# Attention and two MoE layers on one core: a new order of the attention's tasks, in which TensorE keeps its kind of tile

## The chip, the cores and the metric

The kernel runs on one core of one Trainium2 chip. The metric is device time in microseconds (us), from the start to the end of one execution. Five engines work side by side, each with an instruction queue of its own that it executes in order: TensorE (PE, with its weight loads PEld), VectorE (DVE), ScalarE (ACT), GpSimd (POOL) and SyncE (SP), which in this kernel issues nearly all the transfers. They wait for each other through semaphores.

## The reference

Attention over 4 batches, 8 heads, 576 positions and 64 columns a head, mixed with a memory read through phi, and then two MoE layers on the 2304 tokens. All of it is float32.

```python
scores = np.where(causal, -1e9, scale * q @ k.T)          # causal: strictly above the diagonal
a = np.exp(scores - scores.max(-1)); a /= a.sum(-1) + 1e-09
local = a @ v
q_p = phi(q)                                              # x + 1 where x > 0, else exp(x)
mem_out = (q_p @ M_prev) / (q_p @ z_prev + 1e-06)
g = 1 / (1 + np.exp(-beta))
attn = g * mem_out + (1 - g) * local
x = attn.transpose(0, 2, 1, 3).reshape(2304, 512)
g1 = x @ w_gate; x = (g1 * sigmoid(g1) * (x @ w_val)) @ w_out
h = x @ w_in; out = piecewise(h) @ moe2_w_out              # (h + 1)**2 / 4 between -1 and 1
```

## The kernel before

The program has two parts with a planner each. The first part is the attention, beside the decoding of the first twelve weight units and the early gate and value products of the first three groups of 512 tokens. The second part has the rest of the first MoE layer and the whole second one. A `Plan` collects tasks (engine, duration, priority, what they depend on, which buffers they take), plays them through with an estimated duration for each, and emits the instructions in the order in which its play started them. So every engine's order is fixed when the program is built, and on the chip an engine waits at its next instruction however much later work is ready.

The attention works on 16 pairs of heads (4 batches x 4 pairs, `pair`, L380). For a pair, SyncE loads K with the last 64 positions of Q (`kn`, four DMAs), Q (`qn`, three) and V (`vn`, three), and once a batch z (three) and M (two). TensorE transposes K and Q (`tk`, `tm`, `tq`, L496 to L512), and makes the scores: for the four blocks of 128 rows the scores of both heads side by side, each head on 64 rows of the array (L610, 128, 256, 384 and 512 columns), and the last 64 positions of both heads on the whole array (`qk4`, L640). VectorE masks them and takes the row minimum (L620, L647), ScalarE takes the exponential with its row sum (L627, L658), VectorE adds up and inverts the sums (`r`, L682 and L686), GpSimd multiplies each block by them (L695), and TensorE transposes the scaled blocks on the whole array (`t4`, `t03` to `t01`, `t13` to `t11`, L706 to L746). ScalarE or VectorE copies each transposed bank from PSUM (`copies`, L410 and L417; the table `COPY` says which of them). Beside this, phi of Q is made by ScalarE and VectorE (L529 to L536), its product with z and the sum by GpSimd (L541 to L562), and TensorE transposes it (`tp`, `tp4`, L568). At the end `av0` (L774 and L781, 320 columns a product) and `av1` (256) multiply both heads' M and V, each head on 64 columns of the array, and `x` is written as two float32r parts (L785, L788) and stored.

When a group of 512 tokens has all its pairs stored, its `xh` is loaded again, and the early products `mm<-xh` (L1030, 144 instructions a group) run on the whole array, between the attention's own.

What sets the order are the numbers of `ORDER` and `FIRST_ORDER`, one for each kind of task and added to 100 times the pair's number; `EARLY` for the weight units; `GROUP_AT` and `X_AT` for the early products; and the planner's costs. Of the tasks that are ready and have their buffers, an engine takes the one with the lowest number (`Plan.order`, L154). VectorE's operations that share a port with GpSimd (`port=True`) are played as waiting for it, and all of GpSimd's as waiting for them:

```python
if eng == "DVE" and found["port"]:
    dur += max(0, ends["POOL"] - now)
    ends["DVE"] = now + dur
elif eng == "POOL":
    dur += max(0, ends["DVE"] - now)
    ends["POOL"] = now + dur
```

Of the kernel before, what the change touches and what calls it, by code (L numbers as in the profile page):

```python
# [30 lines left out]
FIRST_PAIRS = 3  # L31
AB, RB1, RB0 = 3, 2, 2
# [4 lines left out]
EARLY = (58464.4906, 31703.8921, 46024.3389, 15376.5891, -67113.9713, 33679.2323, 24516.8779, 64604.3348, 926.9641, 15791.9914, 50392.9186, 34533.2938)  # L37
# [8 lines left out]
GROUP_AT, X_AT = (58101.0278, -5262.7152, 78550.5678), (81713.5868, 13183.1344, -54614.9227)  # L46
# [20 lines left out]
    "load": -13097.6716, "load_v": 55113.6308, "load_z": -18855.7456, "load_M": 38998.1826, "tk": 51026.1438,  # L67
    "tm": -96571.9864, "tq": -19483.9254, "tk.cp": -45495.7399, "tm.cp": -7125.2447, "tq.cp": -15756.7918,
    "min": -42893.5849, "exp": -31473.534, "phi": 250.0948, "w": -55573.7784, "fold": -2977.3896, "nrm":
# [9 lines left out]
}  # L79
FIRST_ORDER = {  # L80
    "load": -35369.7195, "load_v": 11324.0126, "load_z": -39943.6113, "load_M": -1948.6302, "tk": 57244.7662,
    "tm": -20365.3582, "tq": 43517.0557, "tk.cp": -28665.4259, "tm.cp": -32651.252, "tq.cp": -2666.435, "min":
    -17582.8303, "exp": -34662.1945, "phi": 32542.1117, "w": -33941.3334, "fold": -21505.6005, "nrm":
# [9 lines left out]
}  # L93
# [179 lines left out]
def c_pool(n):  # L273
    return 0.835 * n + 250
# [1350 lines left out]
```

## Time and profile before

| | us |
|---|---|
| median of 3 runs (1055.95 to 1058.71) | 1056.94 |
| the profiled execution | 1055.26 |
| its span, first to last instruction | 1053.5 |
| TensorE busy in the span | 1037.8 (99%) |
| VectorE busy | 672.7 (64%) |
| ScalarE busy | 569.5 (54%) |
| GpSimd busy, all of it in the attention | 216.0 (21%) |

The rows further below come from this execution. An engine is busy while it has an instruction in execution; matmuls are pipelined and the ends of theirs are modelled, so that the start of one group to the start of the next tells more of TensorE than the busy time does. "PEclk" is the granted clock of TensorE as a share of full speed. "[1.22 <-DMA qn]" behind a row is how long the engine was idle before it, in us, and what ended that. A score or `av` product appears as two records in the trace, a transposition as one.

### The profile page before, as it was taken

What the parts mean: (1) busy time and instruction counts of PE and PEld (TensorE: products, weight loads), DVE (VectorE), ACT (ScalarE), POOL (GpSimd) and SP (SyncE); (2) the same over time, 40 slices, a digit from 0 to 9 for tenths busy, and PEclk for the clock granted to TensorE, in tenths of its full rate; (3) what the DMA queues carried; (4) which work ended last, traced back from release to release, by engine and by line L of the source; (5) the groups of instructions that cost most, each with busy time, mean ns of one, the idle gap of its engine ahead of it and who ended that gap; (6) DMA issues with size and microseconds to landing.
All of it is one profiled execution on the core that took longest, in us unless ns stands there. A gap on an engine that the chain in (4) does not pass through costs nothing.

```text
span 1053.5 us, 17539 instructions
## 1 busy us (share of the span) xinstructions
PE 1037.8 (99%) x6096; PEld 862.9 (82%) x6096; DVE 672.7 (64%) x1547; ACT 569.5 (54%) x1282; POOL 216.0 (21%) x301
## 2 busy tenths in 40 slices
PE   6899999999999999999999999999999999999998
PEld 4666766767788898888888889999999999899997
DVE  5899787761124677968777776843585767643443
ACT  6898887883222445525353444655564555544443
POOL 7898998992000000000000000000000000000000
PEclk8999999999999999999999999999999999999999
DMA  7794564224596699765869696999679878855422
GB/s 167 181 241 121 169 172 137 91 89 156 199 301 202 214 343 401 227 234 203 315 236 333 208 341 228 362 409 414 245 267 336 310 266 292 285 208 189 166 81 80
DMA packets 172072, 248.10 MB, mean 236 GB/s; under 512 B 72913, under 2 KB 99537, under 8 KB 171985
## 3 DMA queue, kind: packets, MB, share of 16 engines
q1 hardware_dynamic: 170078, 245.64, 68.5%
q10 hardware_dynamic: 1906, 1.35, 0.4%
q8 instruction: 48, 0.79, 0.3%
q14 instruction: 40, 0.32, 0.1%
HBM read 165.15 MB, written 81.79 MB: 234 GB/s over the span
## 4 chain that ended last, share of the span: by engine, by line
PE 95%; ACT 1%; DMA 1%; SPq 1%; POOL 1%; issue 0%; DVE 0%; ACTq 0%; POOLq 0%
PE mm L1030 28%; PE acc L1558 19%; PE mm L1279 17%; PE acc L1374 14%; PE av L781 4%; PE s L610 3%; PE t L729 2%; PE av L774 2%; PE s L640 1%; PE t L746 1%; PE t L706 1%; PE tp L568 1%; DMA qn<-in_q_dram 1%; PE tk L499 1%; ACT a L627 0%; SPq L431 0%
## 5 line engine op out<-in xcount | busy, mean ns | idle before, releaser
L1558 PE MATMUL acc<-wu,h 128*128 128x512 f32 x864 | 210.3, 391 | 0.0
L1030 PE MATMUL mm<-xb,wu 128*128 128x512 f32 (+1 forms) x1008 | 201.1, 359 | 0.0
L1030 PEld LDWEIGHTS mm<-xb,wu 128*128 128x128 f32 x1008 | 170.1, 189 | 28.3
L1558 PEld LDWEIGHTS acc<-wu,h 128*128 128x128 f32 x864 | 157.4, 189 | 29.3
L1279 PE MATMUL mm<-xb,wu 128*128 128x256 f32 x1188 | 153.9, 283 | 0.0
L1279 PEld LDWEIGHTS mm<-xb,wu 128*128 128x128 f32 x1188 | 150.0, 192 | 3.6 <-ACT mm L1350 0.3
L1374 PE MATMUL acc<-h,wu 128*128 128x512 f32 (+1 forms) x720 | 151.8, 368 | 0.0
L1374 PEld LDWEIGHTS acc<-h,wu 128*128 128x128 f32 x720 | 125.8, 189 | 22.4
L1191 ACT CAST h<-t 128x512 fp32r<-128x512 f32 (+1 forms) x140 | 80.6, 579 | 91.3 <-PE acc L1374 37.3
L1194 DVE TENSOR_TENSOR h<-t,h 128x512 fp32r<-128x512 f32 (+1 forms) x140 | 88.3, 635 | 50.3 <-ACT h L1191 49.6
L1263 ACT ACTIVATE t<-mm,half 128x512 f32<-128x512 f32 (+1 forms) x80 | 51.7, 646 | 117.7 <-PE mm L1279 73.4
L1030 PE MATMUL mm<-xh,wu 128*128 128x512 f32 x432 | 107.5, 401 | 0.0
L695 POOL TENSOR_SCALAR a<-a,r,OGP 128x512 f32<-128x512 f32 (+3 forms) x144 | 98.8, 698 | 15.0 <-DVE r L686 10.6
L1269 DVE SCALAR_TENSOR_TENSOR t<-mm,t 128x512 f32<-128x512 f32 (+1 forms) x80 | 50.9, 637 | 75.5 <-ACT t L1266 75.2
L1030 PEld LDWEIGHTS mm<-xh,wu 128*128 128x128 f32 x432 | 79.4, 188 | 18.0 <-issue 0.5
L1078 ACT COPY gvo<-mm 128x512 f32<-128x512 f32 (+1 forms) x80 | 43.0, 543 | 92.6 <-PE mm L1030 81.9
L627 ACT ACTIVATE a<-a,mn 128x256 f32<-128x256 f32 (+3 forms) x128 | 70.9, 556 | 4.8 <-DVE mn L620 4.5
L847 ACT ACTIVATE wA<-raw 128x512 f32<-128x512 f32 x64 | 43.0, 672 | 41.1 <-DMA raw<-in_moe_w_out_dram 18.7
L417 DVE COPY R<-t 128x256 f32<-128x256 f32 (+3 forms) x96 | 35.8, 416 | 41.7 <-PE t L746 35.7
L620 DVE CUSTOM_DVE_ANT_0 a<-s,mask 128x256 f32<-128x256 f32 (+3 forms) x128 | 56.8, 481 | 8.5 <-PE s L610 8.1
L908 ACT CAST wu<-wA 128x512 fp32r<-128x512 f32 x56 | 34.6, 617 | 30.8 <-DVE wA L877 22.4
L852 DVE TENSOR_SCALAR wA<-wA 128x512 f32<-128x512 f32 x68 | 31.0, 456 | 31.0 <-ACT wA L847 30.9
(132 smaller groups left out, 1407.9 us busy)
## 6 DMA issues: line engine op xcount, KB each, us to landing
xb<-ys SPq DMA_DIRECT2D x69, 512.0 KB, 7.7
park<-wu SPq DMA_DIRECT2D x40, 512.0 KB, 7.1
wu<-park SPq DMA_DIRECT2D x40, 512.0 KB, 6.8
xb<-xs SPq DMA_DIRECT2D x32, 512.0 KB, 7.4
gv<-gv SPq DMA_DIRECT2D x32, 512.0 KB, 7.1
ys<-yo SPq DMA_DIRECT2D x31, 512.0 KB, 5.7
gv<-gvo SPq DMA_DIRECT2D x60, 256.0 KB, 3.4
raw<-in_moe_w_out_dram SPq DMA_DIRECT2D x28, 512.0 KB, 6.4
```

What stands on the lines that cost most here:

```text
L620: nc.vector.tensor_tensor_reduce(a, st[f"s{h}{c}"][:, 0:kl], self.mask0[:, 512 - kl:512], -0.125, 3.0e38, ALU.add, ALU.min, mn[:, o:o + 1])
L627: nc.scalar.activation(a, a, AF.Exp, bias=mn[:, o:o + 1], scale=-1.0, accum_out=sm[:, o, 0:1])
L695: nc.gpsimd.tensor_scalar(a, a, st["mn"]["r"][:, o:o + 1], self.OGP[:, n, o:o + 1], op0=ALU.mult, op1=ALU.mult)
L847: nc.scalar.activation(f32(s["F"]), f32(words(s["raw"])[:, :, 1]), AF.Abs)
L1030: nc.tensor.matmul(out, kt_of(unit, pw, kt), x[kt][:, px, cols], start=(kt == 0 and i == 0), stop=(kt == KT - 1 and i == 2))
L1191: nc.scalar.copy(s["h"][:, 0], s["t"])
L1194: nc.vector.tensor_sub(s["h"][:, 1], s["t"], f32(s["h"][:, 0]))
L1263: nc.scalar.activation(mk_t(o), src(), AF.Relu, bias=half, scale=0.5)
L1269: nc.vector.scalar_tensor_tensor(o["t"], src(), 1.0, o["t"], op0=ALU.max, op1=ALU.min)
L1279: nc.tensor.matmul(out, pair["k"](k, pw, j), y["x"][piece][:, px, j], start=first and not (i or j), stop=last and j == 1 and i == 2, skip_ ...
L1374: nc.tensor.matmul(state[m][:, 0:n], l, r, start=(begin and i == 0), stop=(end and i == 2), skip_group_check=True)
L1558: nc.tensor.matmul(state[m], s["h"][:, px, m * P:(m + 1) * P], unit["w"][:, pw], start=(begin and i == 0), stop=(end and i == 2), skip_gro ...
```

## The change

The tables that set the attention's order have new numbers, and so have the copies' engines. The planner knows a kind of tile for each of TensorE's tasks (`form`: 1 for scores, 2 for `av`, 0 for the rest). With `stay` it takes, of the tasks that are ready, the first of the kind it is at, if its number is not more than `stay` above that of the first ready one of another kind; `stay` is 1e9. A change of kind costs 165 ns in the plan (`turn`), and the 150 ns that each score and `av` product cost beside its columns are gone. VectorE's operations on the shared port are now played in two ways: behind GpSimd's operations on two tensors (`port=True` there) they wait until one comes that has a single tensor, or none; behind the others as before. GpSimd's scalings cost 285 instead of 250 ns beside their columns, and a DMA's issue 640 instead of 600.

```diff
+STAY, TURN = 1.0e9, 165
-EARLY = (58464.4906, 31703.8921, 46024.3389, ...
+EARLY = (7014.831, 9462.3219, -44116.6461, ...
-GROUP_AT, X_AT = (58101.0278, -5262.7152, 78550.5678), (81713.5868, 13183.1344, -54614.9227)
+GROUP_AT, X_AT = (-13804.7284, -11763.634, 2577.9887), (-9395.3711, -14855.2931, -18112.8928)
 ORDER = {
-    "load": -13097.6716, "load_v": 55113.6308, "load_z": -18855.7456, "load_M": 38998.1826, "tk": 51026.1438,
+    "load": -6563.114, "load_v": -2708.1865, "load_z": -42493.462, "load_M": -15954.7577, "tk": -16212.2191,
...
-COPY = {"tk": "DVE", "tm": "ACT", "tq": "ACT", "tp": "ACT", "tp4": "ACT", "t4": "DVE", "t03": "ACT", "t02": "ACT",
-        "t01": "DVE", "t13": "DVE", "t12": "ACT", "t11": "ACT"}
+COPY = {"tk": "DVE", "tm": "ACT", "tq": "ACT", "tp": "DVE", "tp4": "ACT", "t4": "ACT", "t03": "DVE", "t02": "DVE",
+        "t01": "ACT", "t13": "ACT", "t12": "ACT", "t11": "ACT"}
...
-        t = self.add("SP", (600 if self.over else 530) * len(times), prio, fn, deps, uses, 0, behind)
+        t = self.add("SP", (640 if self.over else 530) * len(times), prio, fn, deps, uses, 0, behind)
...
-                skipped, found = [], None
+                skipped, found, best = [], None, None
                 while heap:
                     e = heapq.heappop(heap)
                     t = self.tasks[e[1]]
+                    if best is not None and t["prio"][0] > best["prio"][0] + self.stay:
+                        skipped.append(e)
+                        break
...
                     if all(len(free[k]) >= v for k, v in need.items()):
-                        found = t
-                        break
+                        if eng != "PE" or not self.stay or t["form"] == form:
+                            found = t
+                            break
+                        best = best or t
                     skipped.append(e)
+                if found is None and best is not None:
+                    found = best
+                    skipped.remove((best["prio"], best["n"]))
...
+                if eng == "PE":
+                    dur += self.turn * (found["form"] != form)
+                    form = found["form"]
...
+                if eng == "DVE" and found["port"]:
+                    if ends["row"] > now:
+                        shut = found
+                        continue
+                    dur += max(0, ends["POOL"] - now)
+                    ends["DVE"] = now + dur
+                elif eng == "POOL":
+                    if shut is not None and not found["port"]:
+                        ends["DVE"] = now + shut["dur"]
+                        begin(shut, now + shut["dur"])
+                        shut = None
+                    dur += max(0, ends["DVE"] - now)
+                    ends["POOL"] = now + dur
+                    if found["port"]:
+                        ends["row"] = now + dur
...
 def c_two(*cols):
-    return sum(4 * n / 2.4 + 5 for n in cols) + 150
+    return sum(4 * n / 2.4 + 6 for n in cols)
...
 def c_pool(n):
-    return 0.835 * n + 250
+    return 0.835 * n + 285
...
-            t_q = add("PE", c_two(kl), "qk", qk, [t_k, t_S], [*places, i_K, i_S, i_a[0, c], i_a[1, c]])
+            t_q = add("PE", c_two(kl), "qk", qk, [t_k, t_S], [*places, i_K, i_S, i_a[0, c], i_a[1, c]], form=1)
...
-                    [i_o, i_P, i_v, i_M, *(i_R1, i_R0)[rg]])
+                    [i_o, i_P, i_v, i_M, *(i_R1, i_R0)[rg]], form=2)
...
-                    slow={"PE": (15500, 1.7)})
+                    slow={"PE": (15500, 1.7)}, stay=STAY, turn=TURN)
```

TensorE, in the middle of the attention, before: the last transposition of one pair's scaled blocks (`t_2453`), then another pair's scores `s_...<-K,S` (both heads of 512, 384, 256 and 128 columns), with transpositions of scaled blocks (`<-ident,a`) and an early product `mm<-xh` among them.

```order
L729 MATMUL t_2453<-ident,a_2311 128x128 x3
L610 MATMUL s_2460<-K,S 128x512
L610 MATMUL s_2461<-K,S 128x512
L610 MATMUL s_2468<-K,S 128x384
L610 MATMUL s_2469<-K,S 128x384
L746 MATMUL t_2476<-ident,a_2322 128x128
L746 MATMUL t_2476<-ident,a_2317 128x128 x2
L1030 MATMUL mm<-xh,wu 128x512 x6
L610 MATMUL s_2500<-K,S 128x256
L610 MATMUL s_2501<-K,S 128x256
L610 MATMUL s_2508<-K,S 128x128
L610 MATMUL s_2509<-K,S 128x128
L746 MATMUL t_2515<-ident,a_2381 128x128
```

The scores of this pair stand in two runs, with whole-array work between. The same stretch of the pairs now, from a transposition on:

```order
L759 MATMUL t_2505<-ident,a_2349 128x128 x4
L640 MATMUL s_2514<-K,S 128x384
L640 MATMUL s_2515<-K,S 128x384
L640 MATMUL s_2522<-K,S 128x512
L640 MATMUL s_2523<-K,S 128x512
L640 MATMUL s_2533<-K,S 128x256
L640 MATMUL s_2534<-K,S 128x256
L640 MATMUL s_2543<-K,S 128x128
L640 MATMUL s_2544<-K,S 128x128
L1061 MATMUL mm<-xh,wu 128x512 x6
L540 MATMUL tq<-ident,qn 128x128 x4
```

All eight score products of a pair stand in one run, and the whole-array work before and behind them in one run each.

SyncE, behind the first pair's K, before: a weight unit (`raw`), z of the first batch (`zb`, `zh`), K of the second pair (`kn_1`) and its Q (`qn_289`).

```order
L842 DMA raw_267<-in_moe_w_gate_dram 128x4x256
L457 DMA zb_269<-in_z_prev_dram 128x512
L461 DMA zh_271<-in_z_prev_dram 64x4x64 x2
L431 DMA kn_1_195<-in_k_dram 128x4x64 x2
L439 DMA kn_1_195<-in_k_dram 64x2x64
L443 DMA kn_1_195<-in_q_dram 64x2x64
L431 DMA qn_289<-in_q_dram 128x4x64 x2
L446 DMA qn_289<-in_q_dram 128x1x64
```

Now the same queue has z of the first batch and the weight unit first, then z of the second batch (its last piece is the first row here), then V of three pairs (`vn`), and only then the second pair's K and Q (`qn_366`).

```order
L491 DMA zh_276<-in_z_prev_dram 64x4x64 x2
L461 DMA vn_0_197<-in_v_dram 128x4x64 x2
L469 DMA vn_0_197<-in_v_dram 64x2x64
L461 DMA vn_1_198<-in_v_dram 128x4x64 x2
L469 DMA vn_1_198<-in_v_dram 64x2x64
L461 DMA vn_2_199<-in_v_dram 128x4x64 x2
L469 DMA vn_2_199<-in_v_dram 64x2x64
L461 DMA kn_1_195<-in_k_dram 128x4x64 x2
L469 DMA kn_1_195<-in_k_dram 64x2x64
L473 DMA kn_1_195<-in_q_dram 64x2x64
L461 DMA qn_366<-in_q_dram 128x4x64 x2
L476 DMA qn_366<-in_q_dram 128x1x64
```

The second pair's Q moves from the 15th to the 27th DMA of the queue; V comes ahead of it instead of behind.

GpSimd from its first product of the attention (phi `p` by z) to its first scaling of a score block (`a2`, by `r` and `OGP`), before:

```order
L541 TENSOR_TENSOR e_302<-p_325,zb_269 128x512
L545 TENSOR_TENSOR e_302<-p_325,zh_271 128x64
L874 TENSOR_TENSOR wS_332<-wL_336,wS_332 128x512
L552 TENSOR_TENSOR e_302<-e_302 128x9x32
L877 TENSOR_TENSOR wA_296<-wA_296,wS_332 128x512
L541 TENSOR_TENSOR e_343<-p_364,zb_269 128x512
L545 TENSOR_TENSOR e_343<-p_364,zh_271 128x64
L910 TENSOR_TENSOR wu_425<-wA_296,wu_425 128x512
L695 TENSOR_SCALAR a2_372<-a2_372,r_308,OGP_187 128x384
```

And now, with the sum of the first pair (L582) and its norm's product (L592) ahead, and the second pair's product behind:

```order
L571 TENSOR_TENSOR e_286<-p_306,zb_267 128x512
L575 TENSOR_TENSOR e_286<-p_306,zh_269 128x64
L582 TENSOR_TENSOR e_286<-e_286 128x9x32
L582 TENSOR_TENSOR e_286<-e_286 128x9x16
L904 TENSOR_TENSOR wS_355<-wL_362,wS_355 128x512
L907 TENSOR_TENSOR wA_318<-wA_318,wS_355 128x512
L592 TENSOR_TENSOR p_306<-p_306,nrm_380 128x576
L940 TENSOR_TENSOR wu_393<-wA_318,wu_393 128x512
L725 TENSOR_SCALAR a2_349<-a2_349,r_316,OGP_187 128x384
```

Eight operations stand ahead of the first scaling in either order; the second pair's product with z made room for the first pair's remaining phi work.

## Rows read from the trace of the kernel before

**Rows 1.** Stretches: length, busy time (instructions) of PE, PEld, DVE, ACT, POOL, PEclk, DMA.
```profile
8.20:11.60 3.40, 2.91 (x8) 1.83 (x8) 2.44 (x8) 2.33 (x4) 0.00 (x0) 0.50 0.97 202
...
21.90:25.30 3.40, 3.22 (x12) 2.08 (x12) 1.07 (x3) 2.61 (x8) 3.36 (x6) 0.50 0.57 126
...
72.90:247.00 174.10, 173.89 (x1196) 119.56 (x1193) 132.97 (x448) 139.93 (x402) 154.25 (x191) 1.00 0.47 135
247.00:288.40 41.40, 41.40 (x223) 32.30 (x221) 3.09 (x8) 9.57 (x19) 0.00 (x0) 1.00 0.47 169
288.40:322.00 33.60, 33.60 (x147) 27.27 (x146) 10.98 (x24) 6.89 (x12) 0.00 (x0) 1.00 0.88 294
322.00:1053.50 731.50, 727.59 (x4129) 641.06 (x4127) 471.47 (x880) 353.78 (x680) 0.00 (x0) 1.00 0.74 264
```

**Rows 2.** Instructions on `xh`: durations in ns (min/median/max), first and last start.
```profile
L1030 PE MATMUL mm<-xh,wu x432: 387/393/609, 72.9 to 321.7; 128*128 128x512 f32 x144
```

**Rows 3.** Timeline of TensorE, mid attention: start, length (us), line, tiles, records.
```profile
131.74 1.13 PE L610 MATMUL s<-K,S 64*128 64x512 f32 x4
132.80 0.55 PE L729 MATMUL t<-ident,a 128*128 128x128 f32 x3
133.28 0.65 PE L774 MATMUL av<-P,MZ 128*64 128x256 f32 x4
...
134.51 0.92 PE L610 MATMUL s<-K,S 64*128 64x384 f32 x4
135.36 0.55 PE L729 MATMUL t<-ident,a 128*128 128x128 f32 x3
...
144.40 0.60 PE L729 MATMUL t<-ident,a 128*128 128x128 f32 x4
144.84 0.60 PE L568 MATMUL tp<-ident,p 128*128 128x128 f32 x4
...
153.96 0.76 PE L774 MATMUL av<-P,MZ 128*64 128x320 f32 x4
...
156.71 1.66 PE L1030 MATMUL mm<-xh,wu 128*128 128x512 f32 x6
```

**Rows 4.** Timeline of all engines, the start: start, length (us), engine, line, tiles.
```profile
0.74 0.99 SPq L431 DMA_DIRECT2D kn<-in_k_dram  x2
...
10.16 0.62 SPq L446 DMA_DIRECT2D qn<-in_q_dram  x1
...
12.34 1.33 POOL L541 TENSOR_TENSOR e<-p,zb 128x512 f32<-128x512 f32 x1 [4.64 <-DMA qn<-in_q_dram]
...
13.55 0.68 ACT L529 ACTIVATE e<-qn 128x576 f32<-128x576 f32 x1 [0.49 <-DMA qn<-in_q_dram]
...
14.14 0.33 PE L504 MATMUL tm<-ident,kn 128*128 128x128 f32 x1
...
16.33 1.17 PE L510 MATMUL tq<-ident,qn 128*128 128x128 f32 x8 [1.22 <-DMA qn<-in_q_dram]
...
22.08 0.48 PE L504 MATMUL tm<-ident,kn 128*128 128x128 f32 x1 [2.06 <-DMA kn<-in_q_dram]
...
23.98 1.55 PE L610 MATMUL s<-K,S 64*128 64x384 f32 x4
...
24.92 0.55 SPq L446 DMA_DIRECT2D qn<-in_q_dram  x1
...
38.11 0.76 PE L774 MATMUL av<-P,MZ 128*64 128x320 f32 x4 [1.07 <-ACT P L417]
```

**Rows 5.** Waits from 72 to 322 us: total us, times, longest.
```profile
POOL a L695 <- DVE r L686: 6.9, 5, 4.3
```

**Rows 6.** Line 417, the copies: durations in ns (min/median/max), forms.
```profile
L417 DVE COPY R<-t x96: 206/415/692, 28.3 to 283.1; 128x256 f32<-128x256 f32 x32, 128x64 f32<-128x64 f32 x32, 128x384 f32<-128x384 f32 x16, 128x512 f32<-128x512 f32 x16
L417 ACT COPY R<-t x64: 453/480/599, 24.1 to 280.8; 128x384 f32<-128x384 f32 x48, 128x512 f32<-128x512 f32 x16
L417 ACT COPY P<-tp x48: 189/206/603, 32.4 to 249.7; 64x64 f32<-64x64 f32 x32, 128x512 f32<-128x512 f32 x16
```

More of the change, by code (lines that the diff above doesn't have):

```diff
@@ L115, with __init__ @@
     RELEASE = 90
-    def __init__(self, start=None, over=None, lat=None, slow=None):
-        self.slow = slow or {}
+    def __init__(self, start=None, over=None, lat=None, slow=None, stay=0, turn=0):
+        self.slow, self.stay, self.turn = slow or {}, stay, turn
         self.over, self.late = over, {**self.LAT, **(lat or {})}
@@ L130, in inst, with add @@
         return Inst(tag)
-    def add(self, eng, dur, prio, fn, deps=(), uses=(), lat=0, behind=None, port=False):
-        t = {"eng": eng, "port": port, "dur": dur + (self.over.get(eng, 0) if self.over else 0), "prio": (prio, len(self.tasks)), "fn": fn, "uses": list(dict.fromkeys(uses)),
+    def add(self, eng, dur, prio, fn, deps=(), uses=(), lat=0, behind=None, port=False, form=0):
+        t = {"eng": eng, "port": port, "form": form, "dur": dur + (self.over.get(eng, 0) if self.over else 0), "prio": (prio, len(self.tasks)), "fn": fn, "uses": list(dict.fromkeys(uses)),
              "lat": lat + self.late[eng], "next": [], "follow": [], "wait": 0, "n": len(self.tasks)}
@@ L157, in order, with begin @@
         busy = {}
-        ends = {"DVE": 0, "POOL": 0}
+        ends = {"DVE": 0, "POOL": 0, "row": 0}
+        shut = None
         events = []
         out = []
-        now, seq = 0, 0
+        now, seq, form = 0, 0, 0
         def clear(t):
             heapq.heappush(ready[t["eng"]], ((now,) if t["eng"] == "DMA" else t["prio"], t["n"]))
+        def begin(t, until):
+            nonlocal seq
+            heapq.heappush(events, (until, seq, "free", t))
+            heapq.heappush(events, (until + t["lat"], seq + 1, "done", t))
+            heapq.heappush(events, (until + t["lat"] + self.RELEASE, seq + 2, "release", t))
+            seq += 3
         for t in self.tasks:
@@ L203, in order @@
                 dur = found["dur"] * (factor if now < until else 1)
-                if eng == "DVE" and found["port"]:
-                    dur += max(0, ends["POOL"] - now)
-                    ends["DVE"] = now + dur
-                elif eng == "POOL":
-                    dur += max(0, ends["DVE"] - now)
-                    ends["POOL"] = now + dur
+                if eng == "PE":
+                    dur += self.turn * (found["form"] != form)
+                    form = found["form"]
                 out.append(found)
@@ L214, in order @@
                         clear(x)
-                heapq.heappush(events, (now + dur, seq, "free", found))
-                heapq.heappush(events, (now + dur + found["lat"], seq + 1, "done", found))
-                heapq.heappush(events, (now + dur + found["lat"] + self.RELEASE, seq + 2, "release", found))
-                seq += 3
+                if eng == "DVE" and found["port"]:
[8 more added lines that the diff above has]
+                        begin(shut, now + shut["dur"])
+                        shut = None
+                    dur += max(0, ends["DVE"] - now)
+                    ends["POOL"] = now + dur
+                    if found["port"]:
+                        ends["row"] = now + dur
+                begin(found, now + dur)
+            if shut is not None and ends["row"] <= now:
+                ends["DVE"] = now + shut["dur"]
+                begin(shut, now + shut["dur"])
+                shut = None
             assert events, "the plan is stuck"
@@ L896, in number @@
         t2 = plan.add("ACT", c_act(512) + 40, prio, lambda: rest_a(i_L), [t], [i_raw, i_L])
-        t = plan.add("POOL", c_pool2(512), prio, rest_b, [t, t2], [i_L, i_S])
-        return plan.add("POOL", c_pool2(512), prio, lambda: whole(nc.gpsimd), [t], [i_F, i_S])
+        t = plan.add("POOL", c_pool2(512), prio, rest_b, [t, t2], [i_L, i_S], port=True)
+        return plan.add("POOL", c_pool2(512), prio, lambda: whole(nc.gpsimd), [t], [i_F, i_S], port=True)
     def split(self, plan, prio, t, src, dst, n, uses, act=True):
@@ L909, in split @@
                      t, uses)
-        return plan.add(e2, c2, prio, lambda: two.tensor_sub(dst()[:, 1], src(), f32(dst()[:, 0])), [t], uses)
+        return plan.add(e2, c2, prio, lambda: two.tensor_sub(dst()[:, 1], src(), f32(dst()[:, 0])), [t], uses,
+                         port=self.pooled)
     def parked(self, plan, tag, prio, t, old, tile, shape):
```

24 lines of the change are left out of this document (12 added, 12 removed), and 36 rows, old and new, of tables (FIRST_ORDER, ORDER).

## The prediction

> **What bounds the kernel now.** I read the busy times of the stages first, then who holds TensorE in the first of them, then how its instructions follow each other. TensorE executes the attention's program first and the two MoE programs behind it, in one fixed order. The last product of the attention's program (an early product `mm<-xh`) starts at 321.7 us [rows 2], and from 322.0 to the end TensorE is busy 727.6 of 731.5 us [rows 1]. The order tables of the change act on the first program only: in both programs every engine's instructions behind the attention's last ones stand in the same order, so those 731.5 us stay what they are. What can move is the 321.9 us ahead of them.
>
> There TensorE's busy share hides two things. From 72.9 us, where the first `mm<-xh` starts, to 247 us it is busy 173.9 of 174.1 us, and to 322 us without a gap [rows 1, 2]: it waits for nobody. But a busy TensorE need not be working. Take the starts of its groups [rows 3]. Four transpositions on the whole array take 144.84 - 144.40 = 0.44 us, 0.11 each. Three transpositions between a group of scores and an `av` product take 133.28 - 132.80 = 0.48 us where 0.33 is due. A pair of 512-column scores takes 132.80 - 131.74 = 1.06 us and a pair of 384 columns 135.36 - 134.51 = 0.85: 0.21 for each 128 columns of a pair, so 0.84 and 0.63 are work and 0.21 to 0.22 is there in either. `av1` (640 columns a head) takes 134.51 - 133.28 = 1.23 us and `av0` (1536 columns) 156.71 - 153.96 = 2.75: 1.70 ns a column, and 0.15 over. So each run of one kind carries a constant that has nothing to do with its length: 0.21 us a run of scores (tiles of 64 rows), 0.15 a run of `av` (tiles of 64 columns), and 0.15 a run of whole-array work that stands between two others.
>
> **Part 1, TensorE keeps its kind.** Counted in the order of the two programs, the attention's part changes the kind of tile 133 times before and 84 times now. Ahead of the first `mm<-xh` it is 30 and 29, so nothing is gained there; behind it 103 and 55. In runs behind that point: scores 31 to 13, `av` 23 to 16, whole array 50 to 27. With the constants of rows 3 this is 18 x 0.21 + 7 x 0.15 + 23 x 0.15 = 3.8 + 1.05 + 3.45 = 8.3 us. I take 8.2, since the outermost runs touch only one neighbour. TensorE waits for nothing in that stretch, so all of it lies on the path, and the matmuls themselves are the same in number and shape. This term is shown by rows; what is not shown is whether the waits stay away once TensorE is faster (part 3).
>
> **Part 2, the start.** SyncE issues the loads of the second and third pair behind those of three pairs' V and two batches' z. Before, Q of the second pair ends with the 15th DMA, now with the 27th. SyncE needs (24.92 - 0.74) / 38 = 0.64 us a DMA (39 DMAs from the first row to the last of its rows) [rows 4], so that Q is issued 12 x 0.64 = 7.6 us later, at 17.8 instead of 10.2 us. Before, it had landed by 13.55, where ScalarE's wait for it ends; so now by about 21.2. TensorE was through with the first pair's scores at 14.14; it then waited until 16.33 for Q, and until 22.08 for the K of the fourth pair [rows 4]. Now it would stand from 14.1 to about 18.9 for the second K (24th DMA: 0.74 + 23 x 0.64 = 15.5, and 3.4 to land as that Q), and again shortly before 21.2. The second pair's scores started at 23.98; now they need Q at 21.2, its transposition, a copy and two short groups, about 23. By 23.98 TensorE had done 14 transpositions for the third and fourth pair that it now does later, and now does 12 of the first pair's weights and phi that it did later. That is even, within 1 us.
>
> The next place is the fifth pair's Q, 39th before (24.92) and 53rd now: it starts at 0.74 + 52 x 0.64 = 34.0, lands 3.4 us later as the second pair's did (10.16 to 13.55), and its four transpositions end at about 37.9. Counted in the orders, TensorE then has 81 transpositions, 24 score products and a whole `av1` behind it; before, it had 83 transpositions and the same 24 score products when it came to its first `av` product at 38.11 [rows 4]. So the late loads cost nothing by then, and about 1.2 us, an `av1`, are won. GpSimd is the other hand on the start: it stood for 4.6 us until its first product at 12.34 [rows 4]. The new order puts the first pair's phi ahead of a weight's decoding, so that this product may start earlier, but eight operations stand ahead of the first scaling in either order. Bounds: all that the start can win is some 4 us (TensorE's two DMA waits in rows 4, 1.2 and 2.1, and a little of GpSimd's); it loses 4 if the 7.6 us later Q is felt but for those 3.3 us of waits. I take -1.5, nearer to the counts at 23 and 38 us than to either end.
>
> The clock belongs to the start. It was granted at 0.50, the lower of its two levels (1.2 and 2.4 GHz), from 8.2 to 11.6 and from 21.9 to 25.3 us [rows 1]; the second stretch begins in TensorE's wait that ends at 22.08 [rows 4]. I expect two such stretches again, the second some microseconds earlier, and count no difference.
>
> The Trainium skill's page "TensorE: Matmul & The Clock Gate" (Part 1, on the HAM clock gate) says that an idle engine is set back to the lower level. That speaks against this change, since the hole from 14.1 to 18.9 us is a new one. If it cost one more such stretch, 3.4 us at 0.50, the sum would be 1.7 us worse; by the rows alone it is not counted.
>
> **Part 3, new waits behind 72.9 us.** GpSimd scales every score block before TensorE transposes it. From 72.9 to 247 us it is busy 154.25 us of 174.1, 89% [rows 1]; it stands for 19.9 us, of which 6.9 in five waits for the reciprocals on VectorE, the longest 4.3 [rows 5]. Take 8 us out of TensorE and the same 154 us lie in 166: 93%. It still fits, but only if GpSimd's own waits shrink with TensorE's, which hand it the scores. At the other end there is room: GpSimd is done at 247 us, and TensorE has 75 us of work left [rows 1]. The planner now costs GpSimd's scalings 35 ns longer and a DMA 40 ns longer, and no longer adds 150 ns to every score or `av` product but 165 to each change of kind, near the 0.15 to 0.21 of rows 3; a plan with such costs should keep these waits short. Bounds 0 to 6 us; I take +0.8.
>
> **Part 4, the copies.** Per pair, `tp`, `t03` and `t02` go from ScalarE to VectorE, `t4`, `t01` and `t13` the other way. ScalarE: 0.60 + 0.60 + 0.48 leave, 0.48 + 0.60 and four pieces of `t4` come; the 64-column pieces are 0.21, the 256-column ones lie between 0.21 and 0.48, say 0.35: +0.5 us a pair. VectorE: `t4` 2 x 0.42 + 2 x 0.21, 0.69 and about 0.55 leave, 0.69 + 0.69 + 0.55 come: -0.55 [rows 6]. So 8 us over 16 pairs change hands. From 72.9 to 247 us ScalarE is busy 139.9 and VectorE 133.0 of 174.1 us [rows 1]; the lesser part of 8 us added to 80% is hidden by ScalarE's own idle time. I cost it at 0; if that cover were gone it would be the same coupling as in part 3, and lies in its bound.
>
> **Sum.** -8.2 - 1.5 + 0.8 + 0 = -8.9 us. The profiled execution took 1055.26 us (span 1053.5), so 1046.4. The median of the three runs is 1056.94, 1.7 above it, and the changed kernel will be timed as a median too; I set 1047.
>
> **The rivals.** *GpSimd sets the pace (no change).* For it: it is 89% busy [rows 1], and no transposition of a block can start ahead of its scaling. Then TensorE's 8.2 us turn into waits for scalings and the time stays at 1055 to 1057. Against it: GpSimd's 19.9 us of standing are waits for what TensorE starts.
>
> *GpSimd falls behind (slower).* With 1.0e9 as the margin for staying, the planner takes any ready instruction of the same kind before one of another kind however urgent. If a pair's last score thereby comes late, its reciprocal is late and GpSimd stands. Five such waits of 1.4 us are there now; if each of the twelve later pairs had one more, 16.8 us, GpSimd would end at about 264 and TensorE, which now has almost no lead over it, would wait as long: 1055.3 - 8.2 + 16.8 = 1064. It decides from 11 us of added standing on (8.2 + 3.2). Against it: a run of scores of all sizes gives a pair's reciprocal earlier, not later.
>
> *The start is lost.* Q late by 7.6 us is felt but for 3.3 us of it: +4.3, so 1055.3 - 8.2 + 4.3 = 1051, still faster. *The change does not do what it says*: its count of changes of kind is read off the program, so I give that no chance.
>
> **How the numbers follow.** About 0.3%, 3.2 us, is what timing can tell from no change; the bounds are 1053.8 and 1060.1. My forecast (1043 to 1050) 0.60; a start or waits that eat half of the gain (1050 to 1053.8, the lost start among them) 0.19; GpSimd's pace 0.12; GpSimd behind 0.09. Faster 0.79, same 0.12, slower 0.09. The low end is the sum with the start at -4 and no new waits, 1055.3 - 12.2 = 1043, less 1 for the runs' spread; the high end 1055 leaves out some 0.15 above it.
>
> **What would show it.** The first product on `xb` starts at about 313 us instead of 321.9; from it to the end it is again 731 to 732 us. In rows like rows 3 a run of a pair's scores in all four sizes takes 0.84 + 0.63 + 0.42 + 0.21 = 2.1 us and 0.2 over, once. The first `mm<-xh` starts between 70 and 74 us. TensorE's waits for `a` behind 73 us sum to under 2 us. I am wrong if the early products start at 73 us and the last ends after 318, with waits for scalings or copies between; or if the first one starts after 76 us.

## The result, and the profile after

The changed kernel takes 1047.27 us (median of 6 runs, 1045.31 to 1049.55), the kernel before 1056.83 beside it: a ratio of 0.9908, 95% interval 0.9896 to 0.992. The profiled execution took 1048.08 us, its span is 1046.2. The forecast was 1047.

The stretches, as in [rows 1] (length, busy time and instructions of PE, PEld, DVE, ACT, POOL, granted clock, DMA share, GB/s):

```profile
19.50:26.40 6.90, 6.08 (x22) 4.99 (x24) 3.00 (x8) 3.71 (x11) 6.90 (x10) 0.51 0.57 129
74.60:247.00 172.40, 171.97 (x1213) 128.16 (x1211) 131.93 (x413) 143.22 (x433) 156.12 (x192) 1.00 0.50 147
247.00:281.00 34.00, 34.00 (x200) 26.51 (x199) 2.79 (x5) 9.86 (x27) 0.00 (x0) 1.00 0.46 156
314.20:1046.20 732.00, 727.84 (x4129) 641.49 (x4128) 470.84 (x880) 354.38 (x680) 0.00 (x0) 1.00 0.74 264
```

The early products, which were at 72.9 to 321.7 us [rows 2]:

```profile
L1061 PE MATMUL mm<-xh,wu x432: 387/393/608, 74.6 to 314.0; 128*128 128x512 f32 x144
```

The first product on `xb` starts at 314.2 instead of 321.9 us; the rest takes 732.0 instead of 731.5. From the first to the last early product it is 239.4 instead of 248.8 us: 9.4 gained there, 1.7 lost ahead of it. In that stretch TensorE idles 0.43 us up to 247 us and not at all after, and no product of its shows a wait for another engine.

TensorE in the middle of the attention, a whole pair's scores and another pair's, as in [rows 3] (start, length, line, tiles, records):

```profile
135.66 0.27 PE L738 MATMUL t<-ident,a 128*128 128x128 f32 x1
135.87 2.43 PE L640 MATMUL s<-K,S 64*128 64x512 f32 x16
138.22 1.24 PE L670 MATMUL s<-K,QZ 128*128 128x288 f32 x4
...
149.44 2.43 PE L640 MATMUL s<-K,S 64*128 64x512 f32 x16
151.80 0.66 PE L759 MATMUL t<-ident,a 128*128 128x128 f32 x4
```

All four sizes stand in one group (the row names the largest) and take 138.22 - 135.87 = 2.35 us, and 2.36 the second time: 2.1 and once 0.2 over, as forecast. GpSimd's waits for the reciprocals were 6.9 us in five [rows 5]; what is left of them, and the weight loads that waited for a scaled block, from 72 us on (total, times, longest):

```profile
POOL a L725 <- DVE r L716: 0.8, 2, 0.5
PEld t L759 <- POOL a L725: 1.1, 2, 0.8
PEld t L776 <- POOL a L725: 0.5, 1, 0.5
```

TensorE at the start, which answers to [rows 4]:

```profile
6.80 1.06 PE L529 MATMUL tk<-ident,kn 128*128 128x128 f32 x4
...
10.92 3.30 PE L640 MATMUL s<-K,S 64*128 64x512 f32 x16
18.71 0.30 PE L534 MATMUL tm<-ident,kn 128*128 128x128 f32 x1 [4.49 <-DMA kn<-in_q_dram]
...
20.32 1.12 PE L598 MATMUL tp<-ident,p 128*128 128x128 f32 x4 [0.84 <-POOL p L592]
...
21.44 1.06 PE L540 MATMUL tq<-ident,qn 128*128 128x128 f32 x4
...
25.84 2.01 PE L640 MATMUL s<-K,S 64*128 64x384 f32 x8
```

The second K is waited for until 18.7 us (forecast 18.9) and Q's transpositions start at 21.44 (forecast 21.2). But the second pair's scores start at 25.84 instead of about 23: the clock is granted at 0.51, its lower level, for 6.9 us instead of 3.4 (first rows above).

### The profile page after: what moved, and what is told of

Its sections match the earlier page's. It is cut to its first block, busy times and chain, and to the rows that moved or that the text cites. A ratio compares the mean times of both kernels' runs of the same rounds, so it can differ in the third digit from the quotient of the medians.

```text
span 1046.2 us, 17568 instructions
## 1 busy us (share of the span) xinstructions
PE 1031.7 (99%) x6096; PEld 869.8 (83%) x6096; DVE 671.2 (64%) x1499; ACT 573.6 (55%) x1330; POOL 217.7 (21%) x301
## 4 chain that ended last, share of the span: by engine, by line
PE 92%; DVE 2%; DMA 2%; ACT 2%; POOL 1%; issue 0%; SPq 0%; DVEq 0%; ACTq 0%
PE mm L1061 27%; PE acc L1589 19%; PE mm L1310 17%; PE acc L1405 13%; PE av L811 3%; PE s L640 3%; PE t L759 2%; PE av L804 1%; PE s L670 1%; DMA ys<-yo 1%; PE t L776 1%; ACT a L657 1%; PE tp L598 1%; PE tq L540 1%; DMA xs<-x 1%; POOL a L725 1%
## 5 line engine op out<-in xcount | busy, mean ns | idle before, releaser
L725 POOL TENSOR_SCALAR a<-a,r,OGP 128x256 f32<-128x256 f32 (+3 forms) x144 | 99.7, 702 | 7.1 <-DVE r L716 1.7
L811 PEld LDWEIGHTS av<-R,vn 128*64 128x64 f32 x448 | 32.2, 137 | 21.3
```

The source lines that it names most:

```text
L725: nc.gpsimd.tensor_scalar(a, a, st["mn"]["r"][:, o:o + 1], self.OGP[:, n, o:o + 1], op0=ALU.mult, op1=ALU.mult)
L811: nc.tensor.matmul(o[halves[h], c0:c1], st["vn"][:, kc, h], r, start=False, stop=i == len(terms) - 1, tile_position=(0, h * 64), skip_grou ...
```

## The experiments

The theory: the gain is the changes of kind taken away, each worth the half of 0.21 + 0.15 us on TensorE. The rival: it came from the searched order of loads and waits, or from the new picture of VectorE and GpSimd. A second question is where the start's -1.5 us went. Below, "the changed kernel" without a run named is its median 1047.27; once more beside the last runs it had 1046.71.

**The price of a change of kind.** Two kernels have the same added work, one inside the runs of scores, the other amid whole-array work.

```diff
                 out = [psum(f"s{h}{c}", places[h]) for h in range(2)]
+                if c < 3:
+                    nc.tensor.transpose(out[0][:, kl:kl + P], self.ident, self.ident)
```

> The changed kernel with 48 extra whole-array transpositions (identity by identity, 128x128, into columns of a score bank that nobody reads), one ahead of each pair of score products of 384, 256 and 128 columns. The order of everything else stays. They cut the runs of scores: 157 changes of kind instead of 84, 73 more, 55 of them behind the first early product. Theory (a change of kind costs time on TensorE, half of 0.21 + 0.15 us): 48 x 0.11 = 5.3 us of work, behind the first early product 27 x 0.21 + 28 x 0.15 = 9.9 us of changes, ahead of it 18 changes, up to 3.2 us as far as no wait there hides them. So 1047.3 + 15 to 18.4 = 1062 to 1066. Rival (changes of kind are free and the gain came from the new order of loads and waits): only the work, 1052.5.

```diff
             t = psum("tm", i_tm)
+            for j in range(1, 4):
+                nc.tensor.transpose(t[:, j * P:(j + 1) * P], self.ident, self.ident)
```

> The changed kernel with the same 48 extra transpositions, but three beside each of the 16 transpositions of K's last rows, amid other whole-array work: still 84 changes of kind. Theory and rival alike: 48 x 0.11 = 5.3 us, 1051.5 to 1052.6 (somewhat less where they stand in a wait of the start). The difference to the kernel with the same work inside the runs of scores is the price of 73 changes: 10 to 13 us by the theory, 0 by the rival.

Measured: 1061.04 us (ratio to before 1.0037, 1.0024 to 1.005) and 1048.30 (0.9919, 0.9907 to 0.9931). The difference, 12.7 us for 73 changes, is 0.175 us a change; the rival's 0 is excluded. Behind the first early product alone, where no product of TensorE waits for another engine in either, it is 251.6 us to the last one (76.0 to 327.6) and 241.8 (72.9 to 314.7). Six more of the added transpositions stand there in the first, 0.65 us, so 55 changes are 9.2 us: 0.167 each. (The first kernel is 1 us short of its range: the price is a little under the 0.18 expected, and ahead of the first early product 18 changes and 15 transpositions, 4.8 us by these prices, delay it by 1.4 to 2.3 us only.) A pair's scores in the first of them:

```profile
140.08 1.13 PE L642 MATMUL s<-K,S 64*128 64x512 f32 x4
141.14 0.33 PE L640 MATMUL s<-ident 128*128 128x128 f32 x1
141.40 0.92 PE L642 MATMUL s<-K,S 64*128 64x384 f32 x4
142.24 0.33 PE L640 MATMUL s<-ident 128*128 128x128 f32 x1
142.50 0.70 PE L642 MATMUL s<-K,S 64*128 64x256 f32 x4
143.13 0.33 PE L640 MATMUL s<-ident 128*128 128x128 f32 x1
143.39 0.49 PE L642 MATMUL s<-K,S 64*128 64x128 f32 x4
143.81 1.24 PE L672 MATMUL s<-K,QZ 128*128 128x288 f32 x4
```

The same scores take 143.81 - 140.08 = 3.73 instead of 2.35 us. Three transpositions are 0.33, so six changes are 1.05: again 0.175 each, with no wait shown in any row. The Trainium skill's page "TensorEngine Tiling (Array Packing)" (Key Properties) says that changing the tiling mode drains TensorE; the rows agree in that each change costs time, and give the price. That it is a drain, they don't show.

Against expectation the second kernel was only 1.0 us above the changed one, not 4 to 5. Behind its first early product (72.9 to 314.7 us) it is 241.8 us, 2.4 to 3.0 more than the changed kernel's two profiles, for 27 added transpositions (2.9). Ahead of it are 21 more, and yet it comes 0.8 to 1.7 us earlier than in the changed kernel; what gave that back at the start isn't shown.

**The rule alone, and the tables alone.** The kernel before with only the planner's kind of tile:

```diff
+STAY, TURN = 1.0e9, 165
...
+                        if eng != "PE" or not self.stay or t["form"] == form:
+                            found = t
+                            break
+                        best = best or t
...
-    return sum(4 * n / 2.4 + 5 for n in cols) + 150
+    return sum(4 * n / 2.4 + 6 for n in cols)
```

> The kernel before with one part of the change: the planner's kind of tile (stay 1e9, turn 165, and the scores' and av products' 150 ns gone). The tables, the copies' engines, the picture of VectorE beside GpSimd and the other costs stay those of before. TensorE's order then has 80 changes of kind in the attention's part (before 133, changed kernel 84). Theory (the gain is the changes taken away, whatever order takes them): 9.0 us of them gone, 1057.3 - 9 = 1048.3, plus new waits, since the tables were not made for it: 1047.5 to 1052, and the waits show as idle time of TensorE. Rival (the searched tables and the picture of VectorE made the gain): 1055 to 1059.

And the changed kernel without it:

```diff
-                    slow={"PE": (15500, 1.7)}, stay=STAY, turn=TURN)
+                    slow={"PE": (15500, 1.7)}, stay=0, turn=0)
```

> The changed kernel without the planner's kind of tile (stay 0, turn 0); tables, copies, picture and the other costs are the changed ones. 136 changes of kind instead of 84. Theory: 52 changes more are 8.7 us, so 1047.3 + 8.7 = 1056, plus waits of an order that was not searched: 1055.5 to 1060. Rival (tables and picture made the gain): 1045 to 1050.

Measured: 1072.54 us (1.0148, 1.0134 to 1.0162) and 1081.19 (1.023, 1.0216 to 1.0244). Both theories missed both. The first has fewer changes (80) than the changed kernel and is 15.8 us slower than the kernel before. Its GpSimd, with the wait ahead of the row, and its TensorE show why:

```profile
269.04 1.28 POOL L553 TENSOR_TENSOR e<-p,zb 128x512 f32<-128x512 f32 x1 [36.72 <-DVE p L548]
...
309.33 5.56 POOL L707 TENSOR_SCALAR a<-a,r,OGP 128x512 f32<-128x512 f32 x9 [34.85 <-DVE r L698]
```

```profile
231.29 25.34 PE L1042 MATMUL mm<-xh,wu 128*128 128x512 f32 x108
...
270.94 33.84 PE L1042 MATMUL mm<-xh,wu 128*128 128x512 f32 x144
304.71 1.77 PE L622 MATMUL s<-K,S 64*128 64x512 f32 x8
...
329.81 3.69 PE L1042 MATMUL mm<-xb,wu 128*128 128x512 f32 x15
337.82 7.37 PE L1042 MATMUL mm<-xb,wu 128*128 128x512 f32 x20 [4.31 <-DMA xb<-xs]
```

A rule that stays as long as anything of the kind is ready takes 108 and then 144 early products in one go, while transpositions and scores of the last pairs stand behind them. GpSimd stands for 36.7 and 34.9 us, and when it is done there are no early products left to cover the last pair's chain, nor the load of `xb`. The first `xb` product starts at 329.8 (before 321.9), and from there to the end it is 739.1 us (731.5). In the kernel without the rule GpSimd's last waits read the same, and TensorE has 132 early products in one go there too, without any rule of kind (the kernel before has them from 248.85 us, when GpSimd is done):

```profile
249.14 30.94 PE L1061 MATMUL mm<-xh,wu 128*128 128x512 f32 x132
```

```profile
286.58 3.94 POOL L725 TENSOR_SCALAR a<-a,r,OGP 128x256 f32<-128x256 f32 x6 [33.55 <-ACT R L447]
332.37 5.57 POOL L725 TENSOR_SCALAR a<-a,r,OGP 128x256 f32<-128x256 f32 x9 [40.23 <-ACT a L657]
```

The changed kernel has such long runs of early products too (108 and 144), but here are its rows of the end of GpSimd's last operations and the start of the first of them:

```profile
237.49 5.54 POOL L725 TENSOR_SCALAR a<-a,r,OGP 128x256 f32<-128x256 f32 x9
```

```profile
243.68 25.34 PE L1061 MATMUL mm<-xh,wu 128*128 128x512 f32 x108
```

GpSimd is through with all pairs at 243.0, and then they begin. So it takes the tables and the rule together to place the long runs of early products behind GpSimd's last work. Of the 34 us between the kernel without the rule and the changed one, 52 changes are some 9; TensorE's idle time in the whole span is 16 us more (30.4 against 14.4), and the rest is longer busy time, with the clock granted at 0.5 for 27 us instead of 7. Each half alone (the rule without the new picture, too) is slower than the kernel before.

**The picture of the shared port.**

```diff
-                    if ends["row"] > now:
-                        shut = found
-                        continue
...
-                    if found["port"]:
-                        ends["row"] = now + dur
```

> The changed kernel with the old picture of the port that VectorE and GpSimd share (VectorE's operation no longer waits in the plan until GpSimd comes to a single-tensor operation); kind of tile, tables, copies and costs are the changed ones. 80 changes of kind. Theory: -0.6 us for four changes fewer, and the picture is worth nothing by itself: 1046 to 1049. Rival (the better picture is what keeps GpSimd's and VectorE's waits away): TensorE idles 3 us or more behind 75 us, 1050 or more.

Measured: 1049.66 us (0.9937, 0.9924 to 0.9949), 2.4 above the changed kernel with four changes fewer, a little over the theory's range. TensorE idles 1.5 us from 73.9 to 247 (0.43 in the changed kernel) and 0.7 before the first `xb` product. So the picture, or the order that the plan makes with it, is worth some 2 to 3 us, 1.8 of it seen as TensorE's idle time; not the gain, but not nothing.

**The copies' engines.** The order of the changed kernel, with each copy done by its engine of before:

```diff
-                    (nc.scalar.copy if eng == "ACT" else nc.vector.tensor_copy)(dst(), src())
+                    (nc.scalar.copy if RUNS[name] == "ACT" else nc.vector.tensor_copy)(dst(), src())
```

> The changed kernel with its own order on TensorE, GpSimd and SyncE, but the copies out of PSUM done by the engines that did them before (tp, t03, t02 on ScalarE, t4, t01, t13 on VectorE), at the place in the order that the plan gave them. 8 us go from VectorE to ScalarE and back. Theory (part 4 of the prediction: ScalarE and VectorE have room, the copies' engines are worth nothing by themselves): 1046.5 to 1049, TensorE idle less than 2 us more behind 75 us. Rival (the copies' new engines keep the bound engines free of each other, and are part of the gain): 1050 or more, with TensorE waiting for copies (R, P) behind 75 us.

Measured: 1051.59 us (0.9955, 0.9943 to 0.9967), 4.9 above the changed kernel beside it. The theory fell. The early products run from 77.3 to 317.7 us, so about 3 us are lost ahead of them. The 240.4 us behind are 1.0 to 1.6 more than in the changed kernel's two profiles, but a kernel below with the copies as they are (phi moved too) reaches 240.2 as well, so that part isn't clear of the spread. TensorE ahead of them:

```profile
36.23 0.55 PE L761 MATMUL t<-ident,a 128*128 128x128 f32 x3 [1.09 <-POOL a L727]
...
38.58 0.52 PE L778 MATMUL t<-ident,a 128*128 128x128 f32 x3 [0.75 <-POOL e L584]
...
41.15 0.66 PE L542 MATMUL tq<-ident,qn 128*128 128x128 f32 x4 [1.07 <-DVE mn L652]
```

In the changed kernel the first two are 0.59 and 0.36 us and the third isn't there. The changed kernel's busy times from 26 to 46 us (columns as above, from its second profile, below):

```profile
26.00:46.00 20.00, 18.49 (x139) 13.36 (x138) 17.39 (x55) 19.70 (x64) 17.28 (x22) 1.00 0.69 157
```

ScalarE is busy 19.70 of 20 us there, and VectorE 17.39: there is little room to hide what comes to either. The rival's waits for copies behind 75 us are small (0.2 us for `P`).

**The start: loads, holes, clock.** The second pair's K and Q moved ahead of three pairs' V in SyncE's queue:

```diff
+            if name == "load" and num == 1:
+                pl.last["early"] = 1
...
+        out = [*out[:v], *early, *(t for t in out[v:] if "early" not in t)]
```

> The changed kernel, with the second pair's K and Q (7 transfers) issued ahead of the 9 transfers of three pairs' V; every other queue keeps its order. They land 9 x 0.64 = 5.8 us earlier, K at 12.9 instead of 18.7 us, Q at about 15.4. Theory A (the late loads are what the start lost, against the -1.5 us that was forecast): TensorE no longer waits 4.5 us for K and the second pair's scores start 2 to 4 us earlier; 1043 to 1045.5. Theory B (behind K stands the transposition of the first pair's phi, which waits for GpSimd until 20.3 us whatever the loads do, so that the wait only changes its name): a wait of some 5 us there in its place, the first early product within 0.5 us of 74.6, the time 1046.5 to 1047.8.

Measured: 1046.97 us (0.9905, 0.9891 to 0.9918), in theory B's range: the wait has another name and the same length, until GpSimd has the first pair's phi. The first early product is at 73.1, 1.5 us earlier than in the first profile of the changed kernel (theory B had 0.5 at most) and 0.6 earlier than in the second.

```profile
13.63 0.30 PE L542 MATMUL tm<-ident,kn 128*128 128x128 f32 x1 [0.78 <-DMA kn<-in_q_dram]
...
19.76 1.12 PE L606 MATMUL tp<-ident,p 128*128 128x128 f32 x4 [4.87 <-POOL p L600]
```

The hole filled with transpositions that nobody reads:

```diff
             t = psum("tm", i_tm)
+            for _ in range(38 if num == 1 else 0):
+                nc.tensor.transpose(t[:, P:2 * P], self.ident, self.ident)
```

> The changed kernel with 38 extra transpositions (identity by identity) ahead of the second pair's first one, which fill TensorE's wait from 14.2 to 18.7 us: 38 x 0.109 = 4.1 us. Loads and orders are as they were. Theory A (the start was lost to the clock: 0.51 from 19.5 to 26.4 us, behind that wait): the stretch at 0.5 is gone or shorter, the second pair's transpositions and scores take half as long, and the first early product comes 1 to 3 us earlier; 1044.3 to 1046.3. Theory B (GpSimd's scalings and the loads set the start, and a faster TensorE only waits for them): the clock changes, the time stays at 1047 within 0.5. If filling does nothing to the clock, neither is tested and the time is the same.

Measured: 1046.73 us (0.9903, 0.9888 to 0.9918).

```profile
23.41 1.77 PE L642 MATMUL s<-K,S 64*128 64x384 f32 x8 [0.40 <-ACT S L447]
...
32.34 0.63 PE L529 MATMUL tk<-ident,kn 128*128 128x128 f32 x4 [0.66 <-DMA kn<-in_k_dram]
```

No part is granted 0.5 behind the hole any more, and the second pair's scores start at 23.41 instead of 25.84. Then the fourth pair's K and Q, which SyncE issues as late as before, are waited for, and the first early product starts at 74.1, 0.5 us earlier than in the first profile and 0.4 later than in the second. Theory B on the time, theory A on the clock. The Trainium skill's page "TensorE: Matmul & The Clock Gate" (Part 1) says that an idle engine is set back to the lower level, as weighed in the prediction; this run agrees.

More warm-up products, in the wait ahead of the first transposition:

```diff
-WARM = 8
+WARM = 22
```

> The changed kernel with 22 instead of 8 warm-up products of 128x128 ahead of the first transposition (14 more, 0.11 us each at full clock, in TensorE's wait from 4.8 to 6.6 us). Orders and loads stay. Theory A (the start also lost time to the clock from 6.6 to about 14 us, where the first pair's transpositions took 0.21 us each in the changed kernel's profile, and the length of that stretch differs from run to run): the transpositions at 6.8 take 0.11 to 0.15 us, the first pair's scores end at about 12.5 instead of 14.2, and the first early product starts 1 to 2 us ahead of 74.6; 1045 to 1046.5, with less spread than the changed kernel's 1045.3 to 1049.6. Theory B (waits for loads and for GpSimd take it back): 1046.5 to 1047.8.

Measured: 1046.77 us (0.9904, 0.9891 to 0.9918). The first pair's transpositions take 0.11 us each, but start 2 us later, at 8.80, since the 22 products end late; the first early product is at 73.5, and the time is in theory B's range.

All loads up to the fifth pair reordered, with the 22 products; then the first pair's phi as well:

```diff
+START = ((("SP", "load", 1), ("SP", "load_v", 0)), (("SP", "load_v", 1), ("SP", "load", 5)),
+         (("SP", "load_v", 2), ("SP", "load", 6)), (("SP", "load_z", 4), ("SP", "load", 6)),
+         (("SP", "load_M", 4), ("SP", "load_v", 3)))
...
+                moved = [t for t in out if key(t) == what]
```

> The changed kernel with 22 warm-up products instead of 8, and SyncE's first 50 transfers in another order: the second pair's K and Q ahead of V, V of the second and third pair, z and M of the second batch only behind the loads of the fifth pair. K of the fourth pair is then issued 10 transfers earlier (6 us), the fifth pair's Q 11. All other queues keep their order. Theory A (up to 45 us the start hangs on these loads, since SyncE issues one each 0.64 us): the first early product starts 1.5 to 2.5 us ahead of 74.6; 1044.5 to 1046. Theory B (GpSimd sets the start: the first pair's phi at 20 us, and its scalings after it): 1046 to 1047.5.

```diff
+         (("DVE", "nrm", 0), ("DVE", "mx0", 0)), (("POOL", "pn", 0), ("POOL", None, None))
```

> The kernel of the run with the new load order and 22 warm-up products, and besides the first pair's norm of phi (VectorE, three operations) ahead of four of its maxima and GpSimd's product with it one operation earlier. Theory B of that run (GpSimd and what it waits for set the start): the transposition of phi starts at about 18.6 instead of 19.7 to 20.3, and the first early product another 0.5 to 1.5 us earlier; 1043.5 to 1046. Theory A: no difference to that run, within 0.5.

Measured: 1046.89 us (0.9908, 0.9895 to 0.9921) and 1047.87 (0.9917, 0.9903 to 0.9931); first early products at 74.1 and 73.8. In the first no load is waited for any more, but `tp` still waits 4.86 us for phi, until 19.83. That fits its theory B. In the second it starts at 18.71, as forecast, and nothing comes of it: the time meets neither theory's range (its runs spread from 1045.90 to 1050.86). None of the five kernels with a mended start can be told from the changed one by its time, so no version here beats it. Loads and hole mended together were not tried.

The changed kernel once more:

> The changed kernel as it is, once more, for a second profile beside these runs. If the start's loss was a matter of when the clock rose, its low stretches lie or last otherwise than 6.6 to about 14 and 19.5 to 26.4 us, and the first early product starts elsewhere than at 74.6, by 1 us or more, with the same order; if the order alone sets the start, within 0.3 us of 74.6. Behind the first early product 239.6 us to the last one either way. Time 1045.3 to 1049.6, median about 1047.3.

Measured: 1046.71 us (0.9913, 0.9897 to 0.993). Its profile is of the same program as the one above:

```profile
10.34 2.43 PE L640 MATMUL s<-K,S 64*128 64x512 f32 x16
18.18 0.45 PE L534 MATMUL tm<-ident,kn 128*128 128x128 f32 x1 [5.42 <-DMA kn<-in_q_dram]
...
24.51 1.77 PE L640 MATMUL s<-K,S 64*128 64x384 f32 x8
...
38.01 0.60 PE L540 MATMUL tq<-ident,qn 128*128 128x128 f32 x4
```

```profile
L1061 PE MATMUL mm<-xh,wu x432: 387/393/610, 73.7 to 312.5; 128*128 128x512 f32 x144
```

```profile
16.50:23.30 6.80, 4.54 (x17) 3.85 (x18) 4.12 (x14) 5.38 (x19) 6.35 (x8) 0.50 0.62 142
```

The first pair's scores take 2.43 instead of 3.30 us, the stretch granted at 0.50 lies 3 us earlier and partly in the hole, the second pair's start 1.3 us earlier, and the first early product comes 0.9 us earlier, with the same instructions in the same order. Behind it 238.8 us. Two profiles of one program so differ by 1.5 us at the hand-over to `xb` (312.7 and 314.2), nearly 1 of it from the start.

## Why the prediction was right

*Part 1, the kinds of tile* (-8.2 us): right, and the term that carried the sum. At the 0.167 to 0.175 us measured apart from it, 48 changes behind the first early product are 8.0 to 8.4 us. That stretch shrank by 9.4 us, or 10.0 in the second profile. About 1.1 of this is work that now stands ahead of the first early product (a pair's last scores `s<-K,QZ`, four records or about 1.0 us, and one transposition), where the prediction had the same matmuls behind it; so 8.3 to 8.9 is left for the changes. The same instructions take 238.7 to 240.2 us there in the five kernels with a mended start, so this is known to about 1 us. The rest (732.0 instead of 731.5) was forecast unchanged; it is 731.4 to 732.4 in the profiles of the other runs that keep this order, so the 0.5 is within their spread.

*Part 2, the start* (-1.5 us): the term that was mis-sized. The first early product moved from 72.9 to 74.6 or 73.7 us (the sign named was 70 to 74), less 1.1 of moved work: between +0.6 and -0.3. The loads came as worked out, to 0.3 us (K in part by luck: its last DMA was issued at 16.36 instead of 15.5 us, but took 2.35 us instead of 3.4). What failed is the reckoning at 38 us, on which the gain of "about 1.2 us, an `av1`" rested: the fifth pair's Q transpositions were to end at 37.9. They start at 39.57 and 38.01 in the two profiles and take 0.44 us, so they end at 40.0 and 38.5.

```profile
35.94 0.55 PE L759 MATMUL t<-ident,a 128*128 128x128 f32 x3 [0.59 <-POOL a L725]
...
37.90 0.52 PE L776 MATMUL t<-ident,a 128*128 128x128 f32 x3 [0.36 <-POOL e L582]
...
39.40 0.33 PE L534 MATMUL tm<-ident,kn 128*128 128x128 f32 x1 [0.55 <-ACT R L447]
39.57 0.60 PE L540 MATMUL tq<-ident,qn 128*128 128x128 f32 x4
```

This Q was not late: its last DMA was issued at 34.58 (forecast 34.0), and the last row shows no wait. TensorE came to it late, behind a longer low stretch of the clock and the three waits in these rows, for GpSimd and for a copy. Of the clock the prediction said "I expect two such stretches again [...] and count no difference": the second is 6.9 us instead of 3.4 (6.8 in the second profile, 1.7 of it in the hole itself), and 23 us for the second pair's scores holds only with the hole filled (23.41). The added stretch that was weighed there, 1.7 us, came nearer to the start's loss. But the clock alone is not that loss: with the hole filled and the stretch gone, the time moved by 0.5 us at most. The bound on the gain was also named too narrowly: besides K, phi on GpSimd holds TensorE at 20 us, and the fourth pair's loads come next, so that mending one alone moved the time by 0.5 us at most. How the loss divides among them stays open.

*Part 3, new waits* (+0.8, bounds 0 to 6): about 0. GpSimd's waits for reciprocals fell from 6.9 to 0.8 us, TensorE idles 0.43 us, and GpSimd ends at 243 us. The reason given (a plan with such costs keeps them short) is half of it: the picture of the port is worth 2 to 3 us, and the new tables probably far more, as the rule on the old tables, with the old picture and GpSimd's old costs, takes 1072.5 us.

*Part 4, the copies* (0): not shown right. Undone in the new order they cost 4.9 us, some 3 of it at the start, where ScalarE and VectorE have little idle time to hide them; the forecast had looked at 72.9 to 247 us alone. In the order of before they may be worth less; that was not run.

*The sum.* That 1047 meets 1047.27 is in part luck: the start came out 1.2 to 2.1 us worse than its term and the waits 0.8 better, and the changed kernel's profiled executions are 7.2 and 8.8 us below the one before, their medians 9.6 and 10.0, around the 8.9 of the sum.

*The rivals.* GpSimd falling behind was given 1064 us and 0.09. The changed kernel doesn't show it, but the rule alone does, at 1072.5, and it fits the mechanism named (an urgent score passed over because something of the kind at hand is ready), with the early products as what is taken instead; that those scores were ready is not shown. Against it the prediction had that a run of scores gives its reciprocal earlier, and the waits for reciprocals did shrink; it did not have that the long runs of early products must stand behind GpSimd's last work. GpSimd's pace as the bound is excluded: it is busy 156 of 172.4 us, 91%, and only weight loads of TensorE wait for it, 1.6 us in all.

## What to carry to other kernels

Where the profile shows an engine 99% busy, compare start to start of groups of different lengths: a constant that the length doesn't explain may be time that an order can win back, and a pair of kernels with the same added work at two places prices it. Here a greedy rule in a planner was worth its saving only together with priorities that keep long runs of other work away from the chain that feeds the other engines; test each half alone before crediting either. A new hole at the start should be costed with the clock at its lower level behind it, and with the next two things that are late.

## What the runs showed that was not expected

Two profiles of one program differed by 0.9 us at the first early product. At the second pair's scores it is 1.3 us: 0.3 is there already at 20 us, when phi comes, and the rest fits the clock, granted at 0.50 until 23.3 us in one and until 26.4 in the other. In the first 12.7 us of the first profile the view gives a clock of 1.00, while transpositions take 0.21 us each, as they do where 0.50 is granted:

```profile
6.56:12.70 6.14, 6.12 (x17) 3.77 (x19) 3.23 (x8) 3.80 (x9) 4.07 (x13) 1.00 0.99 233
```

The trace's records of the clock begin only at 12.7 us, so ahead of them the durations, not the clock's column, tell the level. And 38 added transpositions ahead of the second pair, 4.4 us of work, cost nothing measurable (1046.73 against 1047.27), because they stood in a hole.
